# One-bank accumulators, high parts before low parts, and a new order table in a one-core attention and feed-forward kernel

## The chip, the cores and the metric

The kernel runs on 1 core of one Trainium2 chip. The metric is the device time of one execution, in microseconds (us). Three runs of the kernel before gave 842.86, 843.58 and 847.34 us; the median is 843.58. TensorE (PE) multiplies into PSUM, which has banks of 512 float32 columns on 128 partitions. VectorE (DVE) and ScalarE (ACT) read PSUM and write SBUF. GpSimd (POOL) does sums in SBUF. SyncE (SP) only issues transfers (DMAs), and so does ACT for a few.

## The reference

```python
q = softmax(q over d); k = softmax(k over s)          # q, k, v: [8, 8, 576, 64] float32
kv = einsum('bhsd,bhse->bhde', k, v)
x = einsum('bhsd,bhde->bhse', q, kv)                  # -> [4608, 512]
h = x @ w_in                                          # w_in [512, 2048]
g = s * relu(h)**2 + b
return g @ w_out                                      # w_out [2048, 512] -> [4608, 512]
```

## The kernel before

Every operand of a product is split into a high part (rounded to the fast 32-bit matmul format) and a low part (the rest), and a product is three matmuls: high times high, high times low of the weights, low times high. Work goes by blocks of 512 tokens. The last three pairs of blocks use a recursive (Strassen) scheme: seven products of sums of blocks instead of eight. In it the first feed-forward matrix is `product(p, k)` for p = 0 to 23, into three one-bank places U, A and B (`BANK`); A's bank is `qa`, the first half of a two-bank tile `BIG[0]`, whose second bank takes small attention matmuls (`kv`, `y`).

The last pair does the second matrix by seven products too (`half_piece(k, i, j)`, k = 1 to 7, i = 0 to 7 the chunk of 128 hidden rows, j = 0 to 3 the quarter of 128 tokens). Each quarter is 128 x 256 and half a bank, so U, A and B are two banks each: `half_1`, `half_2` and `half_5`, each one tile of two banks. U takes products 1, 6, 7 and 4 one upon the other; between them ACT copies what U holds at that point (`exit_`, line 1728; `exit_21`, line 1751), one copy of 128 x 512 per bank. Product 3 goes on top of 5 in B and ends the kernel; `exit_last(j)` (lines 1756 to 1764) adds each quarter of B to a row in SBUF and sends it with two transfers, one from SP and one from ACT.

In the profile L1260 is a product of the first matrix, L1851 one of the second on whole blocks, and L1686 one quarter's matmul of `half_piece`. L1367 and L1369 are ACT's copy and DVE's sum out of the one-bank places, L858 ACT's copy out of the second bank of `BIG[0]`, L437 the `kv` matmuls there. L1000 loads second-matrix weights that were kept in memory (`w<-w_kept`), L1474 loads kept rows (`t<-r_kept`).

A wait in this kernel is set by tile: an operation that reads a tile waits for the last write to any of its banks that stands before it, and a write waits for the last read.

What runs when is not left to a scheduler: each piece of work is an `Op(engine, cost, due, needs, take, free, gives)`, and `order.run` (line 1996) issues them all in the order of the table `FIRST`, whose entries name the stream to go on with. Engines take their instructions strictly in that order. `idle()` fills planned gaps of PE with matmuls into a tile `unused`.

Of the kernel before, what the change touches and what calls it, by code (L numbers as in the profile page):

```python
# [1 line left out]

# [23 lines left out]
def attention_moe(ctx: ExitStack, tc: tile.TileContext, q, k, v, w_in, w_out, s, b, out):  # L26
# [137 lines left out]
    gpool, xpool, wpool = pool("gpool", 2), pool("xpool", 2), pool("wpool", NFC + 1)  # L164
    wide_, small, ends, qpool, sums_q = pool("wide"), pool("small", 4), pool("ends"), pool("qpool", 2), pool("sums", 2)
    dram = ctx.enter_context(tc.tile_pool(name="dram", bufs=1, space=bass.MemoryType.DRAM))
    ps = ctx.enter_context(tc.tile_pool(name="ps", bufs=1, space=bass.MemoryType.PSUM))


    tiny.tile([P, 32], F32, name="before", tag="before", bufs=1)  # L170
# [1484 lines left out]
    def half_piece(k, i, j):  # L1655
# [7 lines left out]
        if i == 0 and k == 5:  # L1663
            needs += [f"c11 {BACK}"]
# [385 lines left out]
```

## Time and profile before

| | |
|---|---|
| median of 3 runs | 843.58 us (842.86 to 847.34) |
| the profiled execution's own time | 843.64 us |
| its span, first to last instruction | 841.9 us |
| mean granted TensorE clock | 0.996 |
| PE busy | 821.4 us (98%) |
| DVE busy | 635.8 us (76%) |
| ACT busy | 535.4 us (64%) |
| POOL busy | 197.4 us (23%) |
| DMA, mean | 206 GB/s |

The span is divided over five engines that work beside each other; a share of 98% for PE says that its instructions nearly always overlap, since one starts before the one ahead of it has ended. Whether PE really works without a pause is read from the starts of its instructions. The granted clock is 1.00 (2.4 GHz) in every stretch between the first few microseconds and the end of PE's work.

### The profile page before, as it was taken

The page shows a single profiled execution, that of the slowest core. Times are in us where ns is not written, and L with a number is a line of the kernel's source. Part 1 is how long each engine was busy: PE and PEld are TensorE (multiplying, and loading weights), DVE is VectorE, ACT ScalarE, POOL GpSimd, SP SyncE. Part 2 cuts the span into 40 slices and gives each one's busy share as a digit, 9 for nine tenths or more (in the row PEclk, how much of TensorE's full clock was granted, in tenths as well). Part 3 has the DMA queues.
Part 4 walks back from the last instruction along what each step waited for, and adds up shares of the span by engine and source line. Part 5 has one row for each costly group of instructions (what it writes and reads, how often), then busy time and mean ns, then how long its engine had stood idle before and what let it go on. Part 6 is the DMA issues. An engine that isn't in the chain of part 4 may idle for free.

```text
span 841.9 us, 13167 instructions
## 1 busy us (share of the span) xinstructions
PE 821.4 (98%) x4591; PEld 687.9 (82%) x4591; DVE 635.8 (76%) x997; ACT 535.4 (64%) x951; POOL 197.4 (23%) x215
## 2 busy tenths in 40 slices
PE   8899999999999999999999999999999999999995
PEld 7688888878888888788878888788888888889985
DVE  7999996687877698787786897765566857788770
ACT  6999866345464556877876446666563367778820
POOL 1000122544676443233230112221010021110000
PEclk9999999999999999999999999999999999999998
DMA  9967425565988987777879997765498443444103
GB/s 311 359 223 251 98 86 158 148 167 139 252 256 270 252 258 218 232 221 223 239 262 294 367 274 218 192 210 164 130 340 313 174 176 147 162 164 142 51 1 100
DMA packets 152550, 173.41 MB, mean 206 GB/s; under 512 B 68900, under 2 KB 117540, under 8 KB 152356
## 3 DMA queue, kind: packets, MB, share of 16 engines
q1 hardware_dynamic: 151348, 171.73, 65.7%
q10 hardware_dynamic: 1136, 0.85, 0.3%
q8 instruction: 36, 0.59, 0.3%
q14 instruction: 30, 0.25, 0.1%
HBM read 115.34 MB, written 43.04 MB: 188 GB/s over the span
## 4 chain that ended last, share of the span: by engine, by line
PE 81%; DMA 5%; DVE 5%; POOL 3%; ACT 2%; issue 2%; SPq 0%; ACTq 0%; DVEq 0%; POOLq 0%
PE acc L1851 31%; PE q L1260 21%; PE h L1778 12%; PE half L1686 10%; PE qa L1260 3%; DMA r_kept<-zone 2%; DMA area<-in_q_dram 1%; DMA st<-in_moe_w_out_dram 1%; PE qa L437 1%; POOL sum L1132 1%; PE kv L437 1%; DMA area<-in_k_dram 1%; PE xp L873 1%; POOL sum L1126 1%; PE qa L885 1%
## 5 line engine op out<-in xcount | busy, mean ns | idle before, releaser
L1851 PE MATMUL acc<-w,gh 128*128 128x512 f32 x880 | 274.1, 393 | 0.0
L1851 PEld LDWEIGHTS acc<-w,gh 128*128 128x128 f32 x880 | 162.4, 188 | 33.0 <-DVE o L1864 0.2
L1851 PE MATMUL acc<-w,gl 128*128 128x512 f32 x440 | 172.0, 391 | 0.0
L1778 PE MATMUL h<-x,w 128*128 128x512 f32 x576 | 143.5, 392 | 1.1 <-ACT r L1804 0.7
L1778 PEld LDWEIGHTS h<-x,w 128*128 128x128 f32 x576 | 107.0, 188 | 24.2 <-ACT r L1804 1.2
L1851 PEld LDWEIGHTS acc<-w,gl 128*128 128x128 f32 x440 | 82.6, 188 | 18.4 <-DVE gl L1483 0.4
L1260 PE MATMUL q<-w,w 128*128 128x512 f32 x376 | 95.7, 390 | 0.0
L1260 PEld LDWEIGHTS q<-w,w 128*128 128x128 f32 x376 | 70.2, 188 | 15.2 <-ACT zone L1367 0.4
L1804 ACT ACTIVATE r<-h 128x512 f32<-128x512 f32 x48 | 28.6, 595 | 71.0 <-PE h L1778 56.4
L1686 PE MATMUL half<-w 128*128 128x256 f32 x224 | 50.8, 283 | 0.0
L752 POOL TENSOR_TENSOR qe<-qe,qr 128x640 f32<-128x640 f32 x24 | 33.6, 1400 | 69.7 <-DVE qr L748 24.0
L734 POOL TENSOR_TENSOR area<-area,qm 128x640 f32<-128x640 f32 x22 | 32.0, 1462 | 67.4 <-DVE qm L717 40.9
L1369 DVE TENSOR_TENSOR zone<-q,zone 128x512 f32<-128x512 f32 x32 | 22.1, 690 | 33.7 <-ACT zone L1367 21.8
L1171 POOL TENSOR_TENSOR w<-zone,w 128x512 fp32r<-128x512 f32 x16 | 22.9, 1434 | 81.5 <-ACT w L1169 78.0
L1686 PEld LDWEIGHTS half<-w 128*128 128x128 f32 x224 | 37.9, 191 | 0.6
L1260 PE MATMUL q<-x,w 128*128 128x512 f32 x144 | 36.8, 390 | 0.0
L1260 PE MATMUL qa<-x,w 128*128 128x512 f32 x144 | 36.6, 390 | 0.0
L1367 ACT COPY zone<-q 128x512 f32<-128x512 f32 x32 | 18.7, 585 | 24.0 <-PE q L1260 17.1
L858 ACT COPY y<-qa 64x320 f32<-64x320 f32 (+1 forms) x48 | 18.9, 394 | 20.7 <-PE qa L885 10.4
L1260 PEld LDWEIGHTS qa<-x,w 128*128 128x128 f32 x144 | 26.9, 188 | 5.6
L1260 PEld LDWEIGHTS q<-x,w 128*128 128x128 f32 x144 | 26.8, 188 | 5.6
L1686 PE MATMUL half<-w,x 128*128 128x256 f32 x168 | 30.6, 284 | 0.7 <-ACT last L1728 0.7
(295 smaller groups left out, 1731.2 us busy)
## 6 DMA issues: line engine op xcount, KB each, us to landing
w<-w_kept SPq DMA_DIRECT2D x56, 512.0 KB, 6.0
st<-in_moe_w_in_dram SPq DMA_DIRECT2D x16, 512.0 KB, 7.1
st<-in_moe_w_out_dram SPq DMA_DIRECT2D x16, 512.0 KB, 6.9
w_kept<-w SPq DMA_DIRECT2D x16, 512.0 KB, 6.1
zone<-s_kept SPq DMA_DIRECT2D x16, 512.0 KB, 4.3
turned<-area SPq DMA_DIRECT2D x24, 320.0 KB, 3.1
qT<-turned SPq DMA_DIRECT2D x48, 160.0 KB, 4.1
area<-in_q_dram SPq DMA_DIRECT2D x14, 512.0 KB, 6.2
```

The source lines that it names most:

```text
L437: nc.tensor.matmul(kv[h * D:(h + 1) * D, i], kt[:, i, h, n], vt(2 * i + h, n), start=(n == 0), stop=(n == NT - 1))
L734: nc.gpsimd.tensor_tensor(out=qt, in0=qt, in1=bc(qm, [P, 2, NT, D]), op=ALU.subtract)
L752: nc.gpsimd.tensor_tensor(out=qe_, in0=qe_, in1=qr, op=ALU.mult)
L858: nc.scalar.copy(y[half[h], at[a]], x[half[1 - h]])
L1171: nc.gpsimd.tensor_tensor(out=sl, in0=F[1], in1=sh.bitcast(F32), op=ALU.subtract)
L1260: nc.tensor.matmul(BANK[where], w(l)[:, c * P:(c + 1) * P], xs[m][:, c], start=k in (0, 1, 3) and n == 0, stop=n == 5, skip_group_check=True)
L1367: nc.scalar.copy(row(), BANK["U"])
L1369: nc.vector.tensor_tensor(out=row(), in0=BANK[("A", "B", "B")[n]], in1=row(), op=ALU.add)
L1686: nc.tensor.matmul(bank(where, j), g[:, js], w_, start=first and j % 2 == 0 and n == 0, stop=n == 2, skip_group_check=True)
L1778: nc.tensor.matmul(hp_, w[:, j, c, :], x[:, c, :], start=(c == 0 and i == 0), stop=(c == NP - 1 and i == 2))
L1804: nc.scalar.activation(r, hp_, AF.Relu)
L1851: nc.tensor.matmul(acc[blk, j // 2][:, j % 2], g[:, js], w_, start=(f == 0 and i == 0), stop=(f == NFC - 1 and i == 2))
```

## The change

Three things are changed together, and the table `FIRST` is new.

- PSUM is cut into pools that can be closed and opened again. The late two-bank tile `BIG[0]` becomes two one-bank tiles `qa` and `b1`. U in the last stage becomes two one-bank tiles `half_U0` and `half_U1`. B in the last stage is `qa` and `b1` instead of a tile of its own, and A is `half_A`, still one tile of two banks.
- A quarter's three matmuls are two pieces: the two with the high part of the row first, for two quarters (or, in `quarters`, pairs of pieces up to four quarters), then the one with the low part. The high piece needs only ACT's cast (`gh..`, `S1h ..` and so on), the low piece also DVE's subtraction. The groups of chunks per bank in `whole_` are (0,1), (2,3,4), (5,6,7) instead of pairs.
- Product 3's last quarter (j = 3) goes to A's second bank, and what B holds for it is added early (`c12b`). `exit_last` sends quarters 0 and 1 together (one add of 128 x 512, one transfer of 256 KB from SP), quarter 2 alone (128 KB, SP), and only quarter 3 in two halves of 64 KB (SP and ACT).

```diff
-    FIRST = (
-        18, 0, 18, 0, 0, 2, 52, 52, 46, 21, ...
+    FIRST = (
+        ...
-    ps = ctx.enter_context(tc.tile_pool(name="ps", bufs=1, space=bass.MemoryType.PSUM))
+    def banks(name, side):
+        stack = ctx.enter_context(ExitStack())
+        return stack, stack.enter_context(tc.tile_pool(name=name, bufs=1, space=bass.MemoryType.PSUM, side=side, reuse_waits="tile"))
+    _, ps = banks("ps", "left")
+    _, acc_low = banks("ps_acc0", "left")
+    accs_open, acc_top = banks("ps_acc1", "left")
+    two_banks, bigs = banks("ps_big", "right")
...
-                BIG.append(ps.tile([P, 2, 512], F32, name="qa", tag="big"))
-                BANK[where] = BIG[0][:, 0]
+                two_banks.close()
+                _, ones = banks("ps_one", "right")
+                BIG.extend(ones.tile([P, 512], F32, name=n, tag=n) for n in ("qa", "b1"))
+                BANK[where] = BIG[0]
...
+    def quarters(i):
+        for k in (1, 2, 3) if i == 1 else (2, 1):
+            todo = [half_piece(k % 2 or 2, i - (k == 2 or i == 1 and k == 1), j, low) for low in range(2) for j in range(NQ)]
+            for n in range(0, 8, 2):
+                yield chain(*todo[n:n + 2])
-    def half_piece(k, i, j):
+    def half_piece(k, i, j, low):
         if k < 3:
-            needs = [f"g{t}"]
+            needs = [f"g{t}" if low else f"gh{t}"]
+        elif low:
+            needs = [f"{LEFT_[k]} {i}"]
         else:
-            needs = [f"{LEFT_[k]} {i}"] + ([f"{RIGHT_[k]} {i}"] if RIGHT_[k] else [])
-        where = {1: "U", 2: "A", 3: "B", 4: "U", 5: "B", 6: "U", 7: "U"}[k]
+            needs = [f"{LEFT_[k].replace('c', 'h')} {i}"] + ([f"{RIGHT_[k]} {i}"] if RIGHT_[k] else [])
+        where = {1: "U", 2: "A", 3: "B" if j < NQ - 1 else "A", 4: "U", 5: "B", 6: "U", 7: "U"}[k]
...
-            if k < 3:
-                x = ps.tile([P, 2, DO], F32, name=f"half_{k}", tag="acc", bufs=2)
-            else:
-                x = ps.tile([P, 2, 512], F32, name="half_5", tag="big")
-            pq[where] = x[:, 0], x[:, 1]
+            if k == 1:
+                accs_open.close()
+                _, ones = banks("ps_quarters", "left")
+                pq["U"] = [ones.tile([P, 512], F32, name=f"half_U{h}", tag=f"U{h}") for h in range(2)]
+            elif k == 2:
+                t_ = acc_low.tile([P, 2, 512], F32, name="half_A", tag="acc")
+                pq["A"] = t_[:, 0], t_[:, 1]
+            elif k == 5:
+                pq["B"] = BIG
-        for n, (g, w_) in enumerate(((gh, w[:, 0]), (gh, w[:, 1]), (gl, w[:, 0]))):
+        for n, (g, w_) in enumerate([(gl, w[:, 0])] if low else [(gh, w[:, 0]), (gh, w[:, 1])]):
     def second_product():
         def some(k, those):
             for h in (0, 2):
                 for i in those:
-                    for j in (h, h + 1):
-                        yield from half_piece(k, i, j)
+                    for low in range(2):
+                        for j in (h, h + 1):
+                            yield from half_piece(k, i, j, low)
         def whole_(k):
-            for i in range(0, HP, 2):
-                yield from some(k, (i, i + 1))
+            for those in ((0, 1), (2, 3, 4), (5, 6, 7)):
+                yield from some(k, those)
...
         if n == 1:
+            yield Op("DVE", 0.42, due, needs=[f"Q5 {HP - 1} {NQ - 1}"], gives=["c12b"])
+            o = u[:, (NQ - 1) * M2:]
+            nc.vector.tensor_tensor(out=o, in0=bank("B", NQ - 1), in1=o, op=ALU.add)
             return
...
     def exit_last(j):
-        yield Op("DVE", 0.42, due, needs=[f"Q3 {HP - 1} {j}"])
-        o = kept_u(1)[:, j * M2:(j + 1) * M2]
-        nc.vector.tensor_tensor(out=o, in0=bank("B", j), in1=o, op=ALU.add)
-        rows = tokens(B - 1, 0, 1)
+        js = (0, 1) if j == 0 else (j,)
+        yield Op("DVE", 0.69 if j == 0 else 0.42, due, needs=[f"Q3 {HP - 1} {js[-1]}"])
+        o = kept_u(1)[:, j * M2:(j + len(js)) * M2]
+        p = bank("A", j) if j == NQ - 1 else pq["B"][0] if j == 0 else bank("B", j)
+        nc.vector.tensor_tensor(out=o, in0=p, in1=o, op=ALU.add)
+        rows = tokens(B - 1, 0, 1)[:, j:j + len(js)]
+        if j < NQ - 1:
+            yield Op("SP", 0.65, due, dma=(0.35 * len(js),))
+            nc.sync.dma_start(rows, o)
+            return
         for i, (e, eng) in enumerate((("SP", nc.sync), ("ACT", nc.scalar))):
-            yield Op(e, 0.1, due)
-            eng.dma_start(rows[half[i], j], o[half[i]])
+            yield Op(e, 0.65, due, dma=(0.2,))
+            eng.dma_start(rows[half[i]], o[half[i]])
```

The kernel after has the same number of matmuls of every kind (4217 on PE in all). PE's first 3288 of them, DVE's first 761 of 999 instructions, ACT's first 716 of 936 and SP's first 475 of 591 stand in the same order as before; what differs there is only which operation some of them wait for. The order is new from about 616 us on (SP) and in the second products (PE).

**PE and ACT at the last product into U.** PE before, from the end of product 7 into product 4; `half` is U's tile of two banks:

```order
L1686 MATMUL half_6430<-w_1237 128x256
L1686 MATMUL half_6430<-w_back,w_265 128x256 x6
L1686 MATMUL half_6430<-w_554,w_522 128x256 x2
L1686 MATMUL half_6430<-w_554 128x256
L1686 MATMUL half_6430<-w_554,w_522 128x256 x2
L1686 MATMUL half_6430<-w_554 128x256
L1686 MATMUL half_6430<-w_back,w_265 128x256 x6
```

PE after, at the same place; `half_U_6432` is bank 0, `half_U_6433` bank 1:

```order
L1731 MATMUL half_U_6433<-w_1260 128x256 x2
L1731 MATMUL half_U_6432<-w_back,w_283 128x256 x6
L1731 MATMUL half_U_6432<-w_580,w_537 128x256 x4
L1731 MATMUL half_U_6432<-w_580 128x256 x2
L1731 MATMUL half_U_6433<-w_back,w_283 128x256 x6
L1731 MATMUL half_U_6433<-w_580,w_537 128x256 x4
L1731 MATMUL half_U_6433<-w_580 128x256 x2
```

ACT before, its copies out of U ahead of product 4 (L1728) and behind it (L1751):

```order
L1728 COPY last<-half_6430 128x512
L1589 ACTIVATE w_811<-w_927,sb 128x512
L1587 CAST t_5909<-w_265 128x512
L1728 COPY last<-half_6430 128x512
L1587 CAST t_5909<-w_1026 128x512
L1589 ACTIVATE w_1237<-w_1345,sb 128x512
L1535 CAST w_1345<-w_1345 128x256
L1587 CAST t_5909<-w_1345 128x512
L1751 COPY last_7737<-half_6430 128x512 x2
```

ACT after, the same copies (L1775 and L1801):

```order
L1775 COPY last<-half_U_6432 128x512
L1775 COPY last<-half_U_6433 128x512
L1621 ACTIVATE w_964<-w_1034,sb 128x512
L1619 CAST t_5911<-w_1358 128x512
L1567 CAST w_1358<-w_1358 128x256
L1801 COPY last_7741<-half_U_6432 128x512
L1801 COPY last_7741<-half_U_6433 128x512
```

The same 12 matmuls per bank stand there; those of one bank now have a tile of their own, the high ones are drawn together, and each copy reads a tile that the matmuls of the other bank do not write.

**SP at the end.** SP's last transfers before, all to the output:

```order
L1754 DMA out_dram<-last_7737 64x4x256 x2
L1764 DMA out_dram<-last 64x256
L1739 DMA out_dram<-last 512x1x256
L1764 DMA out_dram<-last 64x256 x2
L1743 DMA out_dram<-last 64x4x256 x2
L1764 DMA out_dram<-last 64x256
```

and after:

```order
L1817 DMA out_dram<-last 128x2x256
L1789 DMA out_dram<-last 512x1x256
L1804 DMA out_dram<-last_7741 64x4x256 x2
L1793 DMA out_dram<-last 64x4x256 x2
L1817 DMA out_dram<-last 128x256
L1821 DMA out_dram<-last 64x256
```

Four transfers of 64 KB on SP have become one of 256 KB at the front, one of 128 KB and one of 64 KB at the end; product 4's two (L1754, now L1804) stand behind the first instead of ahead of it.

**SP at 617 us.** The loads for the second matrix before (`w_12` is the weight of hidden chunk 12, `t34` a kept row):

```order
L1474 DMA t34_5909<-r_kept_116 128x512 x2
L1000 DMA w_12_1132<-w_kept_115 128x1024
L1000 DMA w_11_1026<-w_kept_115 128x1024
L1000 DMA w_6_724<-w_kept_115 128x1024
L1000 DMA w_9_927<-w_kept_115 128x1024
L1474 DMA t34_5909<-r_kept_116 128x512
L1867 DMA out_0_dram<-o_5_0_5980 128x1024
L1000 DMA w_8_811<-w_kept_115 128x1024
L1000 DMA w_10_953<-w_kept_115 128x1024
L1867 DMA out_0_dram<-o_5_1_6018 128x1024
L1000 DMA w_2_522<-w_kept_115 128x1024
L1000 DMA w_3_554<-w_kept_115 128x1024
```

and after, behind one kept row and the weight of chunk 12:

```order
L1028 DMA w_6_747<-w_kept_124 128x1024
L1028 DMA w_3_580<-w_kept_124 128x1024
L1028 DMA w_9_938<-w_kept_124 128x1024
L1028 DMA w_13_1198<-w_kept_124 128x1024
L1028 DMA w_2_537<-w_kept_124 128x1024
L1028 DMA w_11_1034<-w_kept_124 128x1024
L1504 DMA t34_5911<-r_kept_125 128x512
L1925 DMA out_0_dram<-o_5_0_6001 128x1024
L1925 DMA out_0_dram<-o_5_1_6024 128x1024
L1028 DMA w_5_668<-w_kept_124 128x1024
L1504 DMA t34_5911<-r_kept_125 128x512
L1028 DMA w_8_823<-w_kept_124 128x1024
```

The weight of chunk 8 has moved behind both output transfers and behind the weights of chunks 3, 13, 2 and 5.

## Rows read from the trace of the kernel before

**Rows 1.** The page: busy time with shares; the chain that ended last by engine

```profile
PE   821.4 (98%) x4591; PEld 687.9 (82%) x4591; DVE 635.8 (76%) x997; ACT 535.4 (64%) x951; POOL 197.4 (23%) x215
...
PE 81%; DMA 5%; DVE 5%; POOL 3%; ACT 2%; issue 2%; SPq 0%; ACTq 0%; DVEq 0%; POOLq 0%
```

**Rows 2.** Windows: length, busy us (count) PE PEld DVE ACT POOL, clock, DMA, GB/s

```profile
610.00:652.00 42.00, 42.00 (x187) 34.75 (x187) 26.36 (x36) 22.02 (x37) 3.33 (x3) 1.00 0.91 326
...
785.00:819.00 34.00, 31.89 (x261) 31.19 (x259) 25.99 (x48) 16.64 (x34) 0.00 (x0) 1.00 0.04 13
...
835.00:838.00 3.00, 0.00 (x0) 0.00 (x0) 0.00 (x0) 0.00 (x0) 0.00 (x0) 0.51 0.96 316
```

**Rows 3.** Timeline of PE, last stage: start, us, what, count, idle before

```profile
805.45 0.28 PE L1686 MATMUL half<-w 128*128 128x256 f32 x1
806.40 0.50 PE L1686 MATMUL half<-w,x 128*128 128x256 f32 x2 [0.68 <-ACT last L1728]
806.74 0.28 PE L1686 MATMUL half<-w 128*128 128x256 f32 x1
...
807.58 0.52 PE L1686 MATMUL half<-w_back,w 128*128 128x256 f32 x3
808.78 0.62 PE L1686 MATMUL half<-w_back,w 128*128 128x256 f32 x3 [0.68 <-ACT last L1728]
...
832.37 0.28 PE L1686 MATMUL half<-w 128*128 128x256 f32 x1
```

**Rows 4.** Timeline of ACT: the copies out of U

```profile
805.76 0.58 ACT L1728 COPY last<-half 128x512 f32<-128x512 f32 x1 [5.82 <-PE half L1686]
...
819.15 0.58 ACT L1751 COPY last<-half 128x512 f32<-128x512 f32 x1 [8.47 <-PE half L1686]
```

**Rows 5.** Waits, 785 to 833 us: engine line, waited for, us, times, longest

```profile
PEld half L1686 <- ACT last L1728: 2.7, 3, 1.0
...
PEld half L1686 <- ACT last L1751: 0.9, 1, 0.9
```

**Rows 6.** Timelines at 393 and 438 us: two banks of one tile

```profile
393.53 0.42 ACT L858 COPY y<-qa 64x320 f32<-64x320 f32 x1 [0.98 <-DVE r L1369]
...
437.68 1.52 PE L1260 MATMUL q<-w,w 128*128 128x512 f32 x6
...
439.54 0.68 PE L437 MATMUL qa<-area 128*64 128x65 f32 x15 [0.34 <-DVE r L1369]
```

**Rows 7.** Chain and timelines of DVE and SP at the end

```profile
832.69 0.42 DVE last L1760
...
813.67 2.49 DVE L1593 TENSOR_TENSOR w<-w,t 128x512 fp32r<-128x512 f32 x4
...
832.69 1.42 DVE L1760 TENSOR_TENSOR last<-half,last 128x256 f32<-128x256 f32 x4 [14.73 <-PE half L1686]
...
833.47 0.49 SPq L1764 DMA_DIRECT2D out_dram<-last  x1
...
837.70 0.81 SPq L1764 DMA_DIRECT2D out_dram<-last  x1
```

**Rows 8.** DMA issues by window: issued 833.4 to 834, then from 837.6

```profile
out_dram<-last SPq DMA_DIRECT2D x1, 64.0 KB, 2.2
...
out_dram<-last SPq DMA_DIRECT2D x1, 64.0 KB, 3.1
```

**Rows 9.** Issues of 614 to 645 and of 631.5; SP and PE there

```profile
w<-w_kept SPq DMA_DIRECT2D x11, 512.0 KB, 8.3
...
w<-w_kept SPq DMA_DIRECT2D x1, 512.0 KB, 8.6
...
631.04 0.93 SPq L1000 DMA_DIRECT2D w<-w_kept  x2
...
634.78 3.04 SPq L1474 DMA_DIRECT2D t<-r_kept  x2
...
641.55 0.61 PE L1851 MATMUL acc<-w,gh 128*128 128x512 f32 x2
```

More of the change, by code (lines that the diff above doesn't have):

```diff
@@ L1 @@
 from contextlib import ExitStack
+from itertools import chain
 import concourse.bass as bass
@@ L166, in attention_moe, with acc_tile, acc_free @@
     dram = ctx.enter_context(tc.tile_pool(name="dram", bufs=1, space=bass.MemoryType.DRAM))
-    ps = ctx.enter_context(tc.tile_pool(name="ps", bufs=1, space=bass.MemoryType.PSUM))
+    def banks(name, side):
[5 more added lines that the diff above has]
+    two_banks, bigs = banks("ps_big", "right")
+    free_accs = [acc_low, acc_top]
+    pool_of = {}
+    def acc_tile(name, at=None):
+        pool = free_accs.pop(0)
+        pool_of[at or name] = pool
+        return pool.tile([P, 2, 512], F32, name=name, tag="acc")
+    def acc_free(at):
+        if at in pool_of:
+            free_accs.append(pool_of.pop(at))
     tiny.tile([P, 32], F32, name="before", tag="before", bufs=1)
@@ L468, in k_stream @@
         kt = by_head(tiles[pr][0])[:, 2 * i:2 * i + 2]
-        kT = ps.tile([P, 2, 512], F32, name=f"kT_{u}", tag="big").rearrange("p a b -> p (a b)")
+        kT = bigs.tile([P, 2, 512], F32, name=f"kT_{u}", tag="big").rearrange("p a b -> p (a b)")
         for n in range(NT):
@@ L581, in q_stream @@
         xh, xl = x_tile(bb)
-        xp = ps.tile([P, 2, 512], F32, name=f"xp_{u}", tag=tag, bufs=bufs)
+        xp = (acc_tile(f"xp_{u}") if tag == "acc" else bigs.tile([P, 2, 512], F32, name=f"xp_{u}", tag=tag))
         for a, src in enumerate((slice(0, HB), slice(HB, S))):
@@ L810, in kv_late @@
         kt, _, vt = tiles[pr]
-        kv = BIG[0][:, 1] if alone else ps.tile([P, 512], F32, name=f"kv_{pr}", tag="sm", bufs=1)
+        kv = BIG[1] if alone else ps.tile([P, 512], F32, name=f"kv_{pr}", tag="sm", bufs=1)
         kv = kv[:, 0:2 * (D + 1)].rearrange("p (u e) -> p u e", u=2)
@@ L1274, in late_pe @@
             if a == LAST:
-                todo = iter(rest) if i == 0 else (half_piece(k % 2 or 2, i - (k == 2 or i == 1 and k == 1), j) for k in ((1, 2, 3) if i == 1 else (2, 1)) for j in range(NQ))
+                todo = iter(rest) if i == 0 else quarters(i)
             else:
@@ L1409, in quadrant @@
                 return
-            yield Op("ACT", 0.64, due, take=["g"] if n else (), needs=[f"S2d {i - 1}", f"s4 {i - 1}"] if n and i and i % 2 == 0 else ())
+            yield Op("ACT", 0.64, due, take=["g"] if n else (), gives=[f"gh{t}"], needs=[f"S2d {i - 1}", f"s4 {i - 1}"] if n and i and i % 2 == 0 else ())
             if n:
@@ L1506, in t_sums @@
             needs.append(f"o{(B - 2) * NFC + BY_FREE[1][START_T]} {NQ - 1}")
+            if i == HP - 1:
+                needs.append("left6 1")
         F = None
@@ L1602, in s1_cast @@
         hi, lo = split_g(lambda: high_1(i), low, (lambda: ROWS["A22", i]) if last else lambda: low().bitcast(F32), sb[:, 4:5])
-        yield Op("ACT", 0.64, due, needs=["2b"] + ([f"s1 {i}", f"Q1 {i}"] if last else [f"S1d {i}"]) + [f"P1 {BACK}"])
+        yield Op("ACT", 0.64, due, needs=["2b"] + ([f"s1 {i}", f"Q1 {i}"] if last else [f"S1d {i}"]) + [f"P1 {BACK}"], gives=[f"S1h {i}"])
         hi()
@@ L1610, in s2_cast @@
         hi, lo = split_g(lambda: high_1(i), lambda: slot("A21", i), lambda: slot("A11", i).bitcast(F32), b_col)
-        yield Op("ACT", 0.64, due, needs=[f"S2d {i}", f"Q5 {i}"])
+        yield Op("ACT", 0.64, due, needs=[f"S2d {i}", f"Q5 {i}"], gives=[f"S2h {i}"])
         hi()
@@ L1624, in s3_cast @@
         nc.vector.tensor_tensor(out=ROWS["S3", i], in0=A22(), in1=S2(), op=ALU.subtract)
-        yield Op("ACT", 0.52, due, needs=[f"Q6 {i}"])
+        yield Op("ACT", 0.52, due, needs=[f"Q6 {i}"], gives=[f"S3h {i}"])
         hi()
@@ L1633, in s4_cast @@
         hi, lo = split_g(lambda: high_2(i), low, lambda: low().bitcast(F32), None)
-        yield Op("ACT", 0.52, due, needs=[f"S4d {i}", f"P5 {BACK}"])
+        yield Op("ACT", 0.52, due, needs=[f"S4d {i}", f"P5 {BACK}"], gives=[f"S4h {i}"])
         hi()
@@ L1642, in a22_cast @@
         hi, lo = split_g(lambda: slot("A11", i), low, lambda: low().bitcast(F32), b_col)
-        yield Op("ACT", 0.64, due, needs=[f"s3 {i}", f"S2c {i}"])
+        yield Op("ACT", 0.64, due, needs=[f"s3 {i}", f"S2c {i}"], gives=[f"A22h {i}"])
         hi()
@@ L1653, in bank @@
         return pq[where][j // 2][:, j % 2 * M2:(j % 2 + 1) * M2]
-    def half_piece(k, i, j):
+    def quarters(i):
[4 more added lines that the diff above has]
+    def half_piece(k, i, j, low):
         t = DUE2 - NFC + 2 * i + (k == 2)
         if k < 3:
-            needs = [f"g{t}"]
-        else:
-            needs = [f"{LEFT_[k]} {i}"] + ([f"{RIGHT_[k]} {i}"] if RIGHT_[k] else [])
-        where = {1: "U", 2: "A", 3: "B", 4: "U", 5: "B", 6: "U", 7: "U"}[k]
-        first = i == 0 and k in (1, 2, 5)
-        if i == 0 and k == 5:
+            needs = [f"g{t}" if low else f"gh{t}"]
+        elif low:
+            needs = [f"{LEFT_[k]} {i}"]
+        else:
+            needs = [f"{LEFT_[k].replace('c', 'h')} {i}"] + ([f"{RIGHT_[k]} {i}"] if RIGHT_[k] else [])
+        where = {1: "U", 2: "A", 3: "B" if j < NQ - 1 else "A", 4: "U", 5: "B", 6: "U", 7: "U"}[k]
+        first = not low and i == 0 and (k in (1, 2, 5) or k == 3 and j == NQ - 1)
+        if not low and i == 0 and k == 5:
@@ L1664, in half_piece @@
             needs += [f"c11 {BACK}"]
-        if i == 0 and k == 3:
-            needs += [f"c22b {j // 2}"]
-        if i == 0 and k in (6, 7, 4):
+        if not low and i == 0 and k == 3:
+            needs += [f"c22b {j // 2}"] + (["c12b"] if j == 2 else ["c11b"] if j == 3 else [])
+        if not low and i == 0 and k in (6, 7, 4):
             needs += [f"{({6: 'u1', 7: 'u2', 4: 'u3'})[k]}- {j // 2}"]
         yield Op(
-            "PE", 0.354, DUE2 - NFC + 2 * i if k < 3 else DUE2 + (k, i)[0], needs=needs, take=["acc"] if i == 0 and k < 3 and j == 0 else (),
-            free=["g"] if k == 2 and j == NQ - 1 else (), gives=[f"Q{k} {i} {j}"] + ([f"Q{k} {i}"] if j == NQ - 1 else [])
+            "PE", 0.12 if low else 0.24, DUE2 - NFC + 2 * i if k < 3 else DUE2 + (k, i)[0], needs=needs, take=["acc"] if first and k < 3 and j == 0 else (),
+            free=["g"] if low and k == 2 and j == NQ - 1 else (), gives=[f"Q{k} {i} {j}"] * low + [f"Q{k} {i}"] * (low and j == NQ - 1)
@@ L1684, in half_piece @@
         js = slice(j * P, (j + 1) * P)
-        for n, (g, w_) in enumerate(((gh, w[:, 0]), (gh, w[:, 1]), (gl, w[:, 0]))):
-            nc.tensor.matmul(bank(where, j), g[:, js], w_, start=first and j % 2 == 0 and n == 0, stop=n == 2, skip_group_check=True)
+        for n, (g, w_) in enumerate([(gl, w[:, 0])] if low else [(gh, w[:, 0]), (gh, w[:, 1])]):
+            nc.tensor.matmul(bank(where, j), g[:, js], w_, start=first and (j % 2 == 0 or k == 3) and n == 0, stop=bool(low), skip_group_check=True)
     def second_product():
@@ L1707, in second_product @@
             for i in range(HP):
-                yield from half_piece(3, i, j)
+                for low in range(2):
+                    yield from half_piece(3, i, j, low)
     def kept_u(n):
@@ L1732, in exit_ @@
         for h in range(2):
-            yield Op("DVE", 0.65, due, needs=[f"Q{q} {HP - 1} {2 * h + 1}"], gives=[f"c22b {h}"] if n else ())
+            yield Op("DVE", 0.65, due, needs=[f"Q{q} {HP - 1} {2 * h + 1}"], gives=[f"c22b {h}"] if n else ["c11b"] if h else ())
             uh = u[:, h * 512:(h + 1) * 512]
@@ L1847, in o_parts @@
             if f == 0 and j % 2 == 0:
-                acc[blk, j // 2] = ps.tile([P, 2, DO], F32, name=f"acc_{blk}_{j}", tag="acc", bufs=2)
+                acc[blk, j // 2] = acc_tile(f"acc_{blk}_{j}", (blk, j // 2))
             js = slice(j * P, (j + 1) * P)
@@ L2016, in attention_moe @@
             + [f(i) for f in (s1_cast, s2_cast, s3_cast, s4_cast, a22_cast) for i in range(HP)]
-            + [exit_(n) for n in range(3)] + [exit_21()] + [exit_last(j) for j in range(NQ)],
+            + [exit_(n) for n in range(3)] + [exit_21()] + [exit_last(j) for j in (0, 2, 3)],
             FIRST,
```

16 lines of the change are left out of this document (11 added, 5 removed), and 184 rows, old and new, of the table FIRST.

## The prediction

> **What bounds the kernel now.** I read the page first. PE is busy 98% of the span and makes 81% of the chain that ended last; DVE and ACT are at 76% and 64% [rows 1]. So the end comes sooner only where PE stands still, or in what follows PE's last matmul. Busy time doesn't show either well: matmuls overlap, so I went to the timeline of PE and looked at starts. In the last stage a matmul of 256 columns starts every 0.12 us: three of them take 0.52 us and one 0.28, so two steps are 0.24 [rows 3]. Four times in that stage PE stops. The second is in [rows 3]: from the start at 805.45 to the one at 806.74 there are three steps, which should take 0.36 us and take 1.29, so 0.93 is lost. At 808.78 and at 819.79 it is 0.94 and 0.93 in the same way, at 795.04 it is 1.02. Each time PE waits for ACT's copy out of U [rows 3, 4], and the copy itself had waited for PE: ACT was idle for 5.82 and 8.47 us ahead of two of the copies [rows 4]. This is a ring of two waits on one tile. A copy of bank 0 waits until bank 1 is complete, then PE waits until the copy is over, and nothing lies beside the 0.58 us of copy.
>
> The windows then show that neither DVE nor ACT is full there: 26.0 and 16.6 us of work in the 34 us from 785 to 819, with the granted clock at 1.00 [rows 2]. Last I read the end. PE's last matmul starts at 832.37 [rows 3], the first of four last adds at 832.69, and the span ends at 841.9, so 9.2 us are adds and transfers [rows 7].
>
> **The change, part by part.**
>
> *U in two tiles.* The copies stay (same count, same size), and so do all matmuls, at the same pace as I take it (see the rivals). What goes is the ring. Bank 0's copy can start when bank 0 is complete; by then PE has the last group's matmuls of bank 1 to do, now 18 (three chunks of six), 18 x 0.12 = 2.2 us, against 0.58 of copy [rows 4]. Bank 1's copy has the 12 matmuls that the next product puts into bank 0, 1.4 us. Both are covered where ACT comes to the copy in time. At the change from product 6 to 7 ACT has seven other operations between the two copies. At its mean of 0.49 us in this stretch (16.64 us for 34, rows 2) they take 3.4 us, so bank 1's copy ends 0.6 + 3.4 + 0.6 = 4.6 us after bank 0 is complete. PE needs bank 1 after 18, 12 (of product 2) and 12 matmuls, 42 x 0.12 = 5.0 us: 0.4 is left. So all four stalls go: 1.02 + 0.93 + 0.94 + 0.93 = 3.8 us. Bounds: 3.8, and 1.9 if at two of the four changes ACT is late by as much as the stall is now.
>
> The two ways to read the stalls differ. By the idle column of PE a stall is 0.68 us [rows 3], four of them 2.8; by weight loads it is 2.7 + 0.9 = 3.6 [rows 5]; by starts 3.8. The last also counts the slower first step after a stop (806.40 to 806.74 is 0.34 for two). The Trainium skill says in "Perfetto Trace Analysis", section "Identifying the Most-Contended Engine", that matmul busy time is no good measure because matmuls are pipelined, and that weight-load time should be used. By that rule this term would be 3.6, by PE's idle column 2.8. The trace agrees that the busy column hides most of it, but its starts give a little more still.
>
> *The late two-bank tile in two.* ACT's copy at 393.53 waited 0.98 us for DVE's sum, which reads the other bank, and PE's `kv` matmul at 439.54 did the same [rows 6]. Six product matmuls from 437.68 take 1.52 us, 0.227 per step, so the next was due at 439.04 and came 0.5 later. With two tiles neither waits for the other bank. What is late next is a kept row from memory on other paths a few microseconds on, so I do not add ACT's wait. I take 0.5; bounds 0 (the row's landing eats it) and 1.5 (both in full).
>
> *High first.* The matmuls of the high part no longer wait for DVE's subtraction. In the last stage PE's stops are all by ACT's copies [rows 5], so there is no wait of this kind to remove. I take nothing; bounds 0 and 0.
>
> *The end.* Before, all four adds wait for the whole of B. After, quarters 0 and 1 are complete 48 matmuls before the end (5.8 us), quarter 2 24 before (2.9 us), and only one add of 0.42 us [rows 7] follows PE. Let E be the start of that add. SP sends about 0.36 us after an add ends (832.69 + 0.42 to 833.47, rows 7), so the last 64 KB are issued at E + 0.8. Landing takes 2.2 us when nothing is ahead and 3.1 us behind other transfers [rows 8]; from the last landing (837.70 + 3.1) to the span's end it is 1.1. So the end is E + 4.1 to E + 5.0. What is ahead: 1920 KB, since SP's order puts quarters 0 and 1 first and the other outputs, product 4's among them, behind. The first is issued at about E - 4.4 and the first packets follow some 1.2 us later; at the 316 GB/s of 835 to 838 [rows 2] 1.97 MB take 6.2 us, to E + 3.0, and the last 0.13 MB 0.4 more; with 1.1 the span ends at about E + 4.6. I take 4.6 against 9.2 now: 4.6 gained, bounds 4.1 and 5.1.
>
> The Trainium skill ("DMA: Bandwidth & Descriptors", "Anatomy of one DMA — SWDGE (gpsimd) path") gives a transfer about 2.0 us plus its bytes at 436 GB/s. By that the last 64 KB would take 2.15 us and the term would be 5.1. The row of the empty queue (2.2) agrees; the row behind a backlog (3.1) does not, and after the change there is a backlog.
>
> *New order of loads.* From 610 to 652 us the DMA engines are busy 0.91 of the time [rows 2], and a weight takes 8.3 us to land [rows 9]. The weight of chunk 8 is issued later than before. SP stands at the second output transfer until the result is there, as before (631.04, the next issue, is right behind it); behind it now come weight 5, a row and weight 8, so weight 8 is issued at about 631.8. Before, the load issued at 631.53 landed 8.6 us later, at 640.1 [rows 9], with 5.6 MB asked for since the last row ahead; now it is one weight more, 0.52 MB at some 390 GB/s (0.52 MB in 1.3 us), so 641.4. PE comes to chunk 8 at 641.55 [rows 9], and 0.5 earlier after the gain above. I take 0.4 lost; bounds 0 and 1.5.
>
> *Sum.* 3.8 + 0.5 + 4.6 - 0.4 = 8.5. The profiled execution had a span of 841.9 and a time of 843.64, 1.74 more; it lies 0.06 over the median. 841.9 - 8.5 = 833.4; with 1.74 this is 835.1 us. The terms' bounds give 843.6 - (3.8 + 1.5 + 5.1) = 833.2 and 843.6 - (1.9 + 0 + 4.1 - 1.5) = 839.1.
>
> **The rivals.**
>
> 1. *A new bound eats the stalls.* DVE has 26.0 of 34 us between 785 and 819 [rows 2]. PE will pass this stretch in 30.2, so DVE is at 86% and in strict order behind ACT's casts; if it is late for the last product by what PE gained, only the end and the 0.5 remain: 843.6 - 4.6 - 0.5 + 0.4 = 838.9. Against it: DVE's last sums of operands end at 816.16 [rows 7], and PE begins the last product, 96 matmuls, 11.5 us before its end, at about 820.9; of these 4.7 us PE takes away 3.8, if DVE gains nothing itself. Chance 0.12.
>
> 2. *The change does not do what it says.* Copies and PE still wait for the whole of U, because a wait is set by something wider than the new tile, and the last adds alone gain: 838.9 as well, or, if the end stays as it is and the stalls go, 843.6 - 3.8 - 0.5 + 0.4 = 839.7. For it: three of the four product changes show exactly the same 0.93 us, which a cause other than the tile could give too. Against it: both waits are between the very two engines and tiles that are split. Chance 0.05.
>
> 3. *Slower: the new order of matmuls costs pace.* 929 matmuls stand in a new order, with four or six of the same kind in a row in place of two and one. If changing between banks or weights in that order makes a step longer, every one of them pays. From 0.010 us more per matmul the whole gain of 8.5 is lost (929 x 0.01 = 9.3); at 0.02 the time would be 835.1 + 18.6 = 853.7. For it: the weight load of each takes 0.19 us and must hide in others. Against it: where before has six in a row, the step is 0.12 as well (807.58, rows 3). Chance 0.03.
>
> 4. *Slower loads.* The third kept row, which now stands ahead of both output transfers, waits for its place as the fourth did (634.78, rows 9). Then weight 8 is issued at about 636 and lands 8.3 to 8.6 later, 644.4, PE stops for 3 us, and the time is 837.7. Chance 0.08.
>
> **How the numbers follow.** My forecast, 835.1, has 0.72. Its own range is 833.2 to 837; rivals 1 and 4 reach to 838.9. I give 833.0 to 839.0 for 8 in 10. A difference of 0.5% (4.2 us) is about what a measurement of this kernel can tell from none; the border is 839.4. The forecast, rival 4, and most of 1 and 2 lie below it: 0.89 faster; 0.07 within 0.5%, for parts of rivals 1 and 2; 0.04 slower, for rival 3 and what I have not thought of.
>
> **What would show it.** Right: PE steps evenly from 757 us to its last matmul, with no idle time behind ACT's copies; ACT's copy of bank 0 starts while PE is still in bank 1; one add follows PE's last matmul, and the span ends 4 to 5 us after it begins. Wrong: PE still stopping some 0.9 us at each product change (rival 2); PE waiting for DVE in the last product (rival 1); steps above 0.12 us (rival 3); a stop at about 641 us that ends with a landing weight (rival 4, or the term of 0.4 mis-sized). If the end takes more than 5.1 us from the last add, the backlog of transfers was under-counted.

## The result, and the profile after

The kernel after took 835.38 us (median of 6 runs, 834.12 to 838.38) against 845.68 us for the kernel before (6 runs, 842.86 to 848.29). The ratio of the two is 0.9883, with a 95% interval of 0.9855 to 0.9911: 1.2% faster. Two later batches gave 0.9911 (0.9897 to 0.9924) and 0.9880 (0.9866 to 0.9893). The forecast was 835.1. The profiled execution has a span of 833.7 us, 8.2 less than the 841.9 of before.

The windows of the profile after, columns as in [rows 2]:

```profile
610.00:652.00 42.00, 41.31 (x183) 33.91 (x182) 24.87 (x35) 22.66 (x38) 3.32 (x3) 1.00 0.90 333
785.00:819.00 34.00, 34.00 (x286) 34.00 (x285) 26.50 (x50) 17.27 (x35) 0.00 (x0) 1.00 0.04 13
```

Between 785 and 819 PE starts 286 matmuls instead of 261 [rows 2]; 25 more at 0.12 us are 3.0 us of stops that are gone from this stretch. In the one from 610 to 652 PE loses 0.7, where it lost nothing.

The chain that ended last, after (start, us, what):

```profile
781.46 11.52 PE half_U L1731 x96
792.98 1.44 PE half_A L1731 x12
794.42 23.04 PE half_U L1731 x192
817.46 5.76 PE qa L1731 x48
823.22 2.88 PE b L1731 x24
826.10 2.89 PE half_A L1731 x24
828.99 0.02 issue
829.01 0.42 DVE last L1812
```

One engine from end to end: 192 matmuls in 23.04 us is 0.12 each, and no copy of ACT's stands between them. Then one add, and the span ends 4.7 us after it begins (9.2 before, [rows 7]). ACT's copies at the last change of product, that answer to [rows 4]:

```profile
803.82 0.59 ACT L1775 COPY last<-half_U 128x512 f32<-128x512 f32 x1 [1.93 <-PE half_U L1731]
805.98 0.59 ACT L1775 COPY last<-half_U 128x512 f32<-128x512 f32 x1 [1.57 <-PE half_U L1731]
```

ACT still waits for PE, but the second copy begins 2.16 us after the first, which is the 18 matmuls of bank 1 in between: each waits for its own bank, and PE for neither. DVE's last adds and SP's last transfers:

```profile
823.26 0.69 DVE L1812 TENSOR_TENSOR last<-qa,last 128x512 f32<-128x512 f32 x1 [6.08 <-PE qa L1731]
826.14 0.42 DVE L1812 TENSOR_TENSOR last<-b,last 128x256 f32<-128x256 f32 x1 [2.19 <-PE b L1731]
829.01 0.42 DVE L1812 TENSOR_TENSOR last<-half_A,last 128x256 f32<-128x256 f32 x1 [2.45 <-PE half_A L1731]
```

```profile
823.98 0.40 SPq L1817 DMA_DIRECT2D out_dram<-last  x1
824.43 0.60 SPq L1789 DMA_DIRECT2D out_dram<-last  x1
825.12 1.37 SPq L1804 DMA_DIRECT2D out_dram<-last  x2
826.54 2.02 SPq L1793 DMA_DIRECT2D out_dram<-last  x2
828.67 0.58 SPq L1817 DMA_DIRECT2D out_dram<-last  x1
829.47 0.49 SPq L1821 DMA_DIRECT2D out_dram<-last  x1
```

The adds stand 2.88 us apart, beside PE. SP issues one transfer after another from 823.98 to 829.25, then waits 0.2 us for the last add, which ends at 829.43, and issues the last 64 KB at 829.47. And the one new stop of PE in the last third of the span, in its timeline at 640 us:

```profile
640.53 0.39 PE L1908 MATMUL acc<-w,gl 128*128 128x512 f32 x1
641.60 0.70 PE L1908 MATMUL acc<-w,gh 128*128 128x512 f32 x2 [0.69 <-DMA w<-w_kept]
```

From start to start this is 1.07 where 0.23 is the pace: 0.84 lost, and released by a weight that lands at 641.5.

By starts, PE's stops behind ACT's copies are 3.8 us less than before, and from the add that follows PE's last matmul to the end of the span it is 4.4 less (9.17 and 4.74). 3.8 and 4.4 are 8.2, and the spans differ by 8.2. The other stops of PE come to about the same, but only in sum: 0.5 less at 438 us, 0.9 more at 640, and further up single stops differ by up to 1.1, both ways (1.10 and 0.24 near 177 us, 0.75 and 1.85 near 345).

### The profile page after: what moved, and what is told of

Read it like the earlier page. It is cut to its first block, busy times and chain, and to the rows that moved or that the text cites. A ratio compares the mean times of both kernels' runs of the same rounds, so it can differ in the third digit from the quotient of the medians.

```text
span 833.7 us, 13140 instructions
## 1 busy us (share of the span) xinstructions
PE 820.3 (98%) x4591; PEld 688.6 (83%) x4591; DVE 635.5 (76%) x997; ACT 537.2 (64%) x951; POOL 197.3 (24%) x215
## 4 chain that ended last, share of the span: by engine, by line
PE 78%; DMA 8%; DVE 6%; POOL 2%; SPq 2%; issue 2%; ACT 1%; POOLq 0%; DVEq 0%; ACTq 0%
PE acc L1908 28%; PE q L1290 22%; PE h L1835 10%; PE half_U L1731 6%; PE qa L1290 3%; DMA w<-w_kept 2%; DMA r_kept<-zone 2%; PE half_A L1731 2%; DMA area<-in_q_dram 2%; PE qa L1731 1%; PE b L1731 1%; DMA raw<-in_v_dram 1%; PE b L462 1%; POOL sum L1160 1%; SPq L448 1%
## 5 line engine op out<-in xcount | busy, mean ns | idle before, releaser
L890 DVE TENSOR_TENSOR y<-b,y 64x320 f32<-64x320 f32 (+1 forms) x48 | 21.7, 452 | 14.0 <-ACT y L886 13.2
L1160 POOL TENSOR_TENSOR sum<-sum 128x256 f32<-128x256 f32 x32 | 30.1, 952 | 0.8
L886 ACT COPY y<-b 64x320 f32<-64x320 f32 (+1 forms) x48 | 18.9, 394 | 16.5 <-PE b L913 13.5
L1731 PE MATMUL half_U<-w 128*128 128x256 f32 x168 | 28.1, 283 | 0.0
```

The costliest lines, as they stand in the source:

```text
L886: nc.scalar.copy(y[half[h], at[a]], x[half[1 - h]])
L890: nc.vector.tensor_tensor(out=y[half[h], at[a]], in0=x[half[h]], in1=y[half[h], at[a]], op=ALU.add)
L1160: adds(out=o, in0=x, in1=y, op=op)
L1731: nc.tensor.matmul(bank(where, j), g[:, js], w_, start=first and (j % 2 == 0 or k == 3) and n == 0, stop=bool(low), skip_group_check=True)
```

## The experiments

Each is the kernel after with one edit, unless said otherwise. Medians stand beside the kernel before in the same batch: 842.0 in the first (u_one, b_one, swap_w8, out_first), 842.25 in the second (hilo, out_small, both, after_again), 842.6 in the third (the rest).

**u_one: U as one tile of two banks again.**

```diff
-                pq["U"] = [ones.tile([P, 512], F32, name=f"half_U{h}", tag=f"U{h}") for h in range(2)]
+                u_ = ones.tile([P, 2, 512], F32, name="half_U", tag="U")
+                pq["U"] = u_[:, 0], u_[:, 1]
```

> The kernel after, with U in the last stage as one tile of two banks again; order and everything else as after. Theory (the ring of waits on U's tile made the four stops of the kernel before): PE stops again for some 0.9 us at three or four of the product changes, each ended by ACT's copy out of U, together 2.8 to 3.8 us; the time is about 838.7 against 835.4 for the kernel after, and the end after the last add stays at 4.7. Rival (the stops went because the high parts go first and the matmuls stand in another order): PE steps evenly, the time is 835.4.

Measured: 838.67 us (838.1 to 840.4, 5 runs), ratio to before 0.9962 (0.9946 to 0.9978). PE's timeline, the rows with idle time before them:

```profile
790.09 0.51 PE L1732 MATMUL half_U<-w,x 128*128 128x256 f32 x2 [0.68 <-ACT last L1776]
794.99 0.39 PE L1732 MATMUL half_U<-w_back,w 128*128 128x256 f32 x1 [0.68 <-ACT last L1776]
804.92 0.51 PE L1732 MATMUL half_U<-w,x 128*128 128x256 f32 x2 [0.68 <-ACT last L1776]
808.01 0.74 PE L1732 MATMUL half_U<-w_back,w 128*128 128x256 f32 x4 [0.68 <-ACT last L1776]
818.36 0.50 PE L1732 MATMUL half_U<-w,w 128*128 128x256 f32 x2 [0.73 <-ACT last L1802]
```

Five stops of 0.83 to 0.89 by starts, 4.2 us, 4.7 with the slower first steps; the end stays at 4.8 us from the last add. The new order and the high parts first are all in this kernel, and the stops are back: the tile makes them. This is shown, and the rival falls. At the change from product 6 to 7 there are two stops here and one in the kernel before; the other places are the same. That the two tiles alone would do it, in the old order of matmuls, was not tried.

**b_one: qa and b1 as one tile of two banks again.**

```diff
-                BIG.extend(ones.tile([P, 512], F32, name=n, tag=n) for n in ("qa", "b1"))
+                b_ = ones.tile([P, 2, 512], F32, name="qa", tag="qa")
+                BIG.extend((b_[:, 0], b_[:, 1]))
```

> The kernel after, with qa and b1 as one tile of two banks again. Theory: two things come back. PE's kv matmuls near 438 us wait for DVE's sum out of the other bank, 0.5 us or a little more; and the first of the last adds waits for the third quarter too, which is 24 matmuls or 2.9 us later, and SP's row of transfers behind it starts as much later, so that the span ends 7 to 7.6 us after the last add begins (4.7 now). The time is 838.5 to 839. Rival (the end is set by the last add and the landing of its own transfer alone): only the waits near 438 come back, 835.9.

Measured: 836.48 us (835.7 to 836.7, 4 runs), ratio 0.9928 (0.9914 to 0.9943). PE at 438 us and in the last product:

```profile
438.88 1.33 PE L462 MATMUL qa<-area 128*64 128x65 f32 x38 [0.34 <-DVE r L1400]
...
818.68 0.50 PE L1732 MATMUL qa<-w,t 128*128 128x256 f32 x2 [0.52 <-DVE last L1780]
821.52 0.50 PE L1732 MATMUL qa<-w,t 128*128 128x256 f32 x2 [0.79 <-DVE last L1786]
824.23 0.39 PE L1732 MATMUL qa<-w_back,w 128*128 128x256 f32 x1 [0.78 <-DVE last L1813]
```

The stop at 438 us is back with 0.50 by starts, the same as in the kernel before [rows 6]. At the end both theories were wrong. The adds do not wait for PE's later quarter; PE waits for DVE instead, three times: 0.68 + 0.94 + 0.94 by starts. It is the ring of U again, with DVE in ACT's place. Three of DVE's adds read B, the early one of quarter 3's share (L1780), one of product 5 (L1786) and that of quarters 0 and 1 (L1813); each waits for the matmuls of product 3 that stand ahead of it in either bank, and PE's next matmul into the tile waits for the add. It costs 2.6 us there, and 0.9 comes back: SP's row of transfers starts 0.7 us after the first last add, as in the kernel after, the last add comes 0.8 later against it, and from there to the end it is 3.9 us instead of 4.7.

**swap_w8: weight 8 loaded where weight 13 stood.** In the table `FIRST`, the entry of chunk 8's load and that of chunk 13's exchanged; SP's order:

```diff
-w_13   (fifth load behind the row)
+w_8
...
-w_8    (behind both output transfers and w_5)
+w_13
```

> The kernel after, with two loads of second-matrix weights exchanged in the order: chunk 8 where chunk 13 stood, and 13 where 8 stood. Theory (PE's stop of 0.9 us at 640.5 is the late landing of weight 8): the stop goes and nothing takes its place, since chunk 13 is multiplied near 666; span 832.8, time 834.5. Rival (the DMA engines are full there and another load is late instead): a stop of 0.5 to 1 us at another chunk between 640 and 670, 835.4.

Measured: 832.91 us (832.6 to 835.1, 4 runs), ratio 0.9893 (0.9875 to 0.9911). There is no stop between 636 and 670 us. But there is none either in another profile of the kernel after (after_again, below), so the run does not decide: the stop comes and goes without the edit.

**out_first: the three outputs that are ready go first.** In `FIRST`, the three SP entries of `exit_(0)`, `exit_(2)` and `exit_21` ahead of that of `exit_last(0)`; SP's order:

```diff
+L1789 DMA out_dram<-last 512x1x256
+L1793 DMA out_dram<-last 64x4x256 x2
+L1804 DMA out_dram<-last_7741 64x4x256 x2
 L1817 DMA out_dram<-last 128x2x256
-L1789 DMA out_dram<-last 512x1x256
-L1804 DMA out_dram<-last_7741 64x4x256 x2
-L1793 DMA out_dram<-last 64x4x256 x2
```

> The kernel after, with SP's three earlier outputs (512 KB of product 1 and 2, two of 256 KB each of products 5 and 7 and of product 4) ahead of the transfer of quarters 0 and 1 in SP's order. Theory (the last landing is late because SP sends 1.5 MB behind quarters 0 and 1, though it was ready by 818): they go out by 822, the last 64 KB find empty queues, land 2.2 us after the issue instead of 3.2, and the span ends 3.7 us after the last add begins instead of 4.7; time 834.4. Rival (the last landing takes its 3 us whatever is ahead): 835.4.

Measured: 832.92 us (831.2 to 834.3, 4 runs), ratio 0.9887 (0.9867 to 0.9906). SP's last transfers, and the landing of the last (issues of 827.9 to 828.0):

```profile
815.13 0.60 SPq L1789 DMA_DIRECT2D out_dram<-last  x1
815.83 1.37 SPq L1793 DMA_DIRECT2D out_dram<-last  x2
817.29 2.56 SPq L1804 DMA_DIRECT2D out_dram<-last  x2
822.51 2.96 SPq L1817 DMA_DIRECT2D out_dram<-last  x2
828.00 0.49 SPq L1821 DMA_DIRECT2D out_dram<-last  x1
```

```profile
out_dram<-last SPq DMA_DIRECT2D x1, 64.0 KB, 2.2
```

The last add begins at 827.55 and the span ends at 831.3: 3.75 us, as expected, 0.95 less than after. The last 64 KB land 2.2 us after their issue, against 3.2 in the kernel after. Whether the time falls by as much is for out_first_again.

**hilo: high and low piece of a quarter side by side again.**

```diff
-                    for low in range(2):
-                        for j in (h, h + 1):
+                    for j in (h, h + 1):
+                        for low in range(2):
                             yield from half_piece(k, i, j, low)
...
-            todo = [... for low in range(2) for j in range(NQ)]
+            todo = [... for j in range(NQ) for low in range(2)]
```

> The kernel after, with the high and the low piece of each quarter next to each other again (high, low, then the next quarter) in all second products of the last pair; every other order as after. Theory (high first gives nothing here, since PE never waited for the low parts): PE steps 0.12 us in either order and stops nowhere behind DVE, time 835.4 within 1 us, measured beside the kernel after in the same batch. Rival (the planned order relies on it: a low part is now needed 0.24 to 0.96 us earlier): PE stops behind DVE between 680 and 820 us, 0.2 to 0.9 us a time, 2 us or more in all, 837.5 or more. Second rival (pace): the step is longer in one of the two orders; 0.005 us more per matmul would be 4.6 us.

Measured: 835.17 us (832.8 to 836.4, 4 runs), ratio 0.9915 (0.9901 to 0.9929). PE's waits from 720 to 829 us:

```profile
PEld half_A L1731 <- DVE gl L1449: 0.8, 2, 0.6
PE half_A L1731 <- DVE gl L1449: 0.4, 1, 0.4
```

Two stops behind DVE's subtraction, 0.54 and 0.23 by starts (1.0 in all with the slower first steps), where the kernel after has none in any of three profiles. The step of a matmul is 0.12 in both orders. So the pace rival falls; high first is worth 0.8 to 1.0 us in this order of the other engines, and the theory (nothing) was wrong by that. In the times, 835.17 and 834.67, it does not show.

**out_small: the same bytes in transfers of 64 KB.**

```diff
-            nc.sync.dma_start(rows, o)
+            for n in range(len(js)):
+                for i in range(2):
+                    nc.sync.dma_start(rows[half[i], n], o[half[i], n])
```

> The kernel after, with quarters 0 and 1 sent by SP as four transfers of 64 KB and quarter 2 as two, instead of one of 256 KB and one of 128 KB; bytes and adds as after. Theory (SP's issuing, 0.65 us a transfer, sets the end): four issues more, SP's last one comes 2.0 to 2.6 us later, and the span ends 6.7 to 7.3 us after the last add begins instead of 4.7; time about 837.7. Rival (the bytes set the end, 2 MB at some 300 GB/s): no change, 835.4.

Measured: 836.3 us (835.0 to 838.4, 4 runs), ratio 0.994 (0.9925 to 0.9956); the kernel after beside it 834.67. SP's last transfers:

```profile
821.10 2.44 SPq L1819 DMA_DIRECT2D out_dram<-last  x4
...
827.78 2.06 SPq L1819 DMA_DIRECT2D out_dram<-last  x2
829.94 0.55 SPq L1823 DMA_DIRECT2D out_dram<-last  x1
```

From the last add (826.13) to the end (833.2) it is 7.1 us, inside the 6.7 to 7.3 expected; the last issue comes 3.8 us after that add instead of 0.5, and the last landing takes 2.2 us. The bytes are the same, so here SP's issuing sets the end. It does not follow that it sets the end in the kernel after. There SP is done with the issue ahead of the last at 829.25, the last comes as soon as its add is over, and what is longer is the landing, 3.2 us, while the DMA engines are still at the bytes sent ahead. The landing of the last 64 KB in out_small and in the kernel after, and the window of 825 to 831.5 us in the kernel after (share of the DMA engines and GB/s stand last):

```profile
out_dram<-last SPq DMA_DIRECT2D x1, 64.0 KB, 2.2
...
out_dram<-last SPq DMA_DIRECT2D x1, 64.0 KB, 3.2
...
825.00:831.50 6.50, 3.98 (x34) 3.77 (x32) 0.85 (x2) 0.00 (x0) 0.00 (x0) 1.00 0.97 300
```

In out_first the same bytes have gone before the last add, and the landing takes 2.2. So in the kernel after it is the bytes in flight that make the last landing long, and SP's row of issues is 0.2 us short of becoming the limit; four issues more make it that.

**late_adds: all quarters of product 3 complete at the end.** Product 3 goes chunk by chunk, with the table `FIRST` to match; the order on PE alone changes.

```diff
-        for j in range(NQ):
-            for i in range(HP):
-                for low in range(2):
+        for i in range(HP):
+            for low in range(2):
+                for j in range(NQ):
                     yield from half_piece(3, i, j, low)
```

> The kernel after, with product 3 taken chunk by chunk over all four quarters instead of quarter by quarter, so that all quarters are complete only with PE's last matmuls, as in the kernel before; adds, transfers and SP's order as after. Theory (the gain at the end comes from the adds that run beside PE, not from fewer transfers): SP's row of transfers begins 0.7 us after PE's end and takes the 5.5 us that it takes after, the last 64 KB land 3.2 later, and the span ends some 10.5 us after the first last add begins, which is as long as before (9.2) or longer; time about 840.5. Rival (seven issues less on SP and ACT are worth half of it): 7 us or less after the first add, 837 or less.

Measured: 839.66 us (837.9 to 843.6, 10 runs), ratio 0.9968 (0.9955 to 0.998). DVE's adds:

```profile
827.58 0.69 DVE L1812 TENSOR_TENSOR last<-qa,last 128x512 f32<-128x512 f32 x1 [11.61 <-PE qa L1731]
828.19 0.41 DVE L1812 TENSOR_TENSOR last<-b,last 128x256 f32<-128x256 f32 x1
828.52 0.41 DVE L1812 TENSOR_TENSOR last<-half_A,last 128x256 f32<-128x256 f32 x1
```

The span ends at 837.8, 10.3 us after the first of them (10.5 expected), one more than before. So with the adds behind PE the gain at the end is gone: the adds beside PE are needed for all of it. What fewer transfers are worth is not shown. The last adds send four transfers in place of eight, four fewer and not seven as I had reckoned, and SP's row behind them is not shorter here: product 4's two now stand in it, which makes eight issues where the kernel before has seven.

**after_again, before_again: the same two kernels, a second profile.**

> The kernel after, unchanged, for a second profile and as the measure of the others in this batch. Theory: no stops in the second products, the end 4.7 us after the last add begins; the stops that a load from memory ends (near 177, 344, 380, 450, 536 and 640 us) come out otherwise by up to 1 us each, and the stop at 640 is between 0 and 1 us. Rival: the stop of 0.85 at 640 is there again to 0.1, a fixed price of the new order of loads.

> The kernel before, unchanged, for a second profile. Theory: the four stops behind ACT's copies of U (1.02, 0.93, 0.94, 0.93 us), the stop of 0.5 at 438 us and the 9.2 us at the end come out the same to 0.1; the stops that a load ends (near 177, 344, 380, 425, 536 us) differ by up to 1 us each. Rival: some of the four stops are chance too.

Measured: after_again 834.67 us (833.3 to 835.4, 4 runs), with no stop at 640 us above 0.05 and 5.0 us from the last add to the end (4.7 expected); before_again 842.4 us (1 run). In before_again PE's stops and the end are these:

```profile
793.73 0.50 PE L1686 MATMUL half<-w_back,x 128*128 128x256 f32 x2 [0.76 <-ACT last L1728]
805.10 0.51 PE L1686 MATMUL half<-w,x 128*128 128x256 f32 x2 [0.68 <-ACT last L1728]
807.47 0.63 PE L1686 MATMUL half<-w_back,w 128*128 128x256 f32 x3 [0.68 <-ACT last L1728]
818.49 0.51 PE L1686 MATMUL half<-w,w 128*128 128x256 f32 x2 [0.68 <-ACT last L1751]
...
831.38 1.42 DVE L1760 TENSOR_TENSOR last<-half,last 128x256 f32<-128x256 f32 x4 [14.73 <-PE half L1686]
```

The four stops, the 0.5 at 438 us and the end (831.38 to 840.6, 9.2) are the same to 0.05; what a load ends is not: the stop of 0.58 near 426 us is gone, that at 344 is 1.26 instead of 0.75.

**both, out_first_again, after_third: a version with both changes of order, and out_first beside after once more.**

> The kernel after with the two changes of order that were tried alone: weight 8 loaded in the place of weight 13, and the three earlier outputs sent ahead of quarters 0 and 1. Theory: the span ends 3.75 us after the last add begins, 0.95 less than after, and PE does not stop at 640 us, 0 to 0.9 less; 1 to 1.9 us below the kernel after in the same batch. Rival (the differences of single profiles are chance landings of loads further up): no more than 0.5 us below it.

> The kernel with the three earlier outputs ahead of quarters 0 and 1 once more, beside the kernel after in one batch. Theory: 3.75 us from the last add to the end of the span, and a median 0.5 to 1.5 us below the kernel after. Rival: chance landings further up hide it, within 0.5 us.

> The kernel after, unchanged, as the measure of the others in this batch: 4.7 us from the last add to the end, about 834.7.

Measured: both 832.72 us (829.6 to 834.9, 5 runs), 1.95 below after_again in its batch, with intervals to before that meet (0.9871 to 0.9909, and 0.9897 to 0.9924). In the last batch out_first_again is 833.21 (831.6 to 834.4, 5 runs) and after_third 832.45 (831.8 to 833.0, 4 runs): no gain. The end is 3.7 and 4.7 us from the last add, as expected, so 1 us is saved at that place; but out_first_again stopped at 450 us for 0.87 (by starts), where after_third did not:

```profile
PE acc L1908 <- DMA w<-w_kept: 0.7, 1, 0.7
```

Neither version is shown to beat the kernel after in time.

## Why the prediction came out right, step by step

- *U in two tiles, 3.8 us.* Right: 3.8 less in the profile, four stops that are the same in both profiles of before, none in three profiles of after, and back in u_one. The reading by starts was the right one; the idle column of PE shows 2.7 + 0.7 in u_one for stops that cost 4.7. It does not hide most of a stop, as the prediction says, but about a quarter (2.8 of 3.8 before). ACT was late nowhere: at the change from product 6 to 7 it ends the copy of bank 1 at 795.0, and PE, which starts product 7 at 794.42, comes to that bank 12 matmuls later, at 795.9. Two details of the ring were wrong and cost the sum nothing. A copy does not wait until the other bank is complete, but for the matmuls of either bank that stand ahead of it in the order: at 806.40 and 819.79 PE stops three matmuls into a group of twelve. And the four stops stand at three places, one at the change from 6 to 7, two at 7 to 4 and one at the end of 4; at the first, ACT was at two casts before its second copy and had not waited for PE.
- *The late tile in two, 0.5 us.* Right in size: 0.50 at 438 us, back in b_one. The bound of 1.5 was far too wide. The term left out the last stage, where the same tile is B: b_one shows 2.6 us of stops there. The kernel before has none at that place, so the split keeps the new order from making them and gains nothing against before.
- *High first, nothing.* Right against the kernel before, but given no room: hilo shows 0.8 to 1.0 us within the new order. I asked only whether such a wait stood in the kernel before, and not whether the new order of the other engines leans on the edit.
- *The end, 4.6 us from the last add.* Right in size (4.7, 5.0 and 4.7 in three profiles), and the working holds in the main. With E for the start of the last add, the transfers ahead were to be through at E + 3.0 and the rest at E + 3.4 (with 1.1 that is 4.5, and I took 4.6). The last of those ahead that has a landing on record, the second L1793, landed at E + 3.1 and the last 64 KB at E + 3.7, with the DMA engines busy 0.97 of the time. Two steps were off: SP sends at once after an add, so that the last issue comes at E + 0.46 instead of E + 0.8, and its row starts at E - 5.0 instead of E - 4.4. That the adds must run beside PE is shown (late_adds). What the working did not ask is whether SP's issues could be the limit; they are not, but only by 0.2 us (out_small). The estimate from the Trainium skill ("DMA: Bandwidth & Descriptors", "Anatomy of one DMA — SWDGE (gpsimd) path"), 2.15 us for 64 KB, comes from a section on transfers that GpSimd issues, and these are SP's. It agrees with the last landing where SP's other outputs are out of the way (2.2 in out_first); in the kernel after it is 3.2, and the term by bounds from the rows was nearer.
- *New order of loads, 0.4 us.* The place is right, and the landing too (641.5 against 641.4 worked out), but not as a fixed price. In three profiles of the kernel after, weight 8 lands at 641.5, 639.9 and 637.9, and PE stops there for 0.84, 0.04 and nothing. Of the other runs with this order of loads, late_adds stops 0.5 and out_first 0.2; two profiles of before, swap_w8 and both stop nowhere there. So with the new order an execution pays between 0 and 0.9 there, and which it is was chance.
- *Sum.* The time, 835.4 against 835.1, agrees better than the working deserves. The gain was to be 8.5; between the two profiles it is 8.2, with stops further up that differ by up to 1.1 each and happen to cancel. By the medians of three batches it is 10.3, 7.6 and 10.2, and the kernel before took 845.68 in the first of them, 2 more than the forecast started from.
- *Rivals.* DVE as the next bound did not come: it ends its sums before PE needs them. Rival 2 falls, since no stop behind ACT's copies is left. The order of matmuls costs no pace. Rival 4 did not come: weight 8 is issued at 631.2, not at 636.

## What to carry to other kernels

Where an accumulator of several banks is drained while it is filled, look at what the wait is set on: if it is the tile, the drain waits for whatever was written ahead of it to any bank, and the filler for the drain. Here each such stop cost 0.9 us for a copy of 0.58. The sign is a copy that waits for the matmuls and is waited for at once. At the end of a kernel, ask two things of the last result: is the queue that sends it free when it is ready, and are the bytes sent ahead of it through. Sending first what is ready first took 1 us off the end in out_first, though no gain in the whole time was shown. And before a stop that a load ends is put down to a change, look at a second profile.

## What the runs showed that was not expected

The same load of 512 KB of weights, issued at 441.7 and at 442.6 us behind the same transfers in the same order, landed 3.9 us later in after_third and 7.9 in out_first_again (5.0 and 7.0 in the other two profiles of the kernel after), and PE's stop behind it is 0 in the one and 0.87 in the other:

```profile
w<-w_kept SPq DMA_DIRECT2D x1, 512.0 KB, 3.9
```

```profile
w<-w_kept SPq DMA_DIRECT2D x1, 512.0 KB, 7.9
```

Runs of one kernel in one batch differ by 1 to 6 us; such landings may be why, but that was not tried, and what decides them stays open.
